# Moving transposes one slot, splitting the first feed-forward pair and reordering one block in an mLSTM and Fourier-mixing kernel

## The chip, the core and the metric

The kernel runs on one core of a Trainium2 chip. The metric is the device time of that core in microseconds, from one launch to its end. The engines are named as the profile names them: PE is TensorE's matrix multiply and PEld its weight load, DVE is VectorE, ACT is ScalarE, POOL is GpSimd, and SP issues the transfers (all of them here).

## The reference

All tensors are float32, with 4 batches, 8 heads, 768 tokens and a head width of 40. The first half is an mLSTM cell, a recurrence over the tokens whose output for each token and head is a gated read of a decaying 40 x 40 state:

```python
C = f_stab * C + i_stab * outer(v_t, k_t);  n = f_stab * n + i_stab * k_t
y[t] = sigmoid(o_t) * (C @ q_t) / max(|n . q_t|, 1)
```

The second half takes the 320 features of each token (8 heads of 40):

```python
u  = x + real(fft(fft(x, axis=seq), axis=feature))
un = (u - mean(u)) / sqrt(var(u) + 1e-6)
out = u + relu(un @ w_ch1) @ w_ch2          # 320 -> 1280 -> 320
```

## The kernel before

The tokens of a batch are cut into six chunks of 128. The mLSTM is computed chunk by chunk, as decayed attention inside a chunk and a state carried between chunks. `mlstm_scores` multiplies the keys and queries of a chunk into two PSUM banks (pool `ps_s`), `mlstm_exp` makes decay weights on ACT, POOL masks them, and `mlstm_weigh` multiplies the two on DVE. I call the PE work of one later chunk (read of the state, scores of the next, product with the values, new state) a chunk block.

The Fourier transform is done with matrices of cosines and sines. `mix_feat` leaves the transform of two chunks in a bank `pu`. Then for each chunk, in the order 0, 5, 1, 4, 2, 3:

- `mix_add` (DVE) adds the transform to x, giving u, and takes mean and variance. Chunks 2 and 3 read the same `pu`, as do 0 and 5, and 1 and 4.
- `mix_center` (ACT) writes u minus its mean into one of two buffers `uc`.
- `mix_turn` (PE, "a turn") transposes it in three 128 x 128 pieces into a bank `put`.
- `mix_turn_out` (ACT) copies that to `uT`, which the feed-forward product reads.

For batches 2 and 3 the banks are fixed by a table: the turns go to banks 3, 3, 3, 3, 2, 3 and the three `pu` sit in banks 3, 2, 2. So the fifth turn (chunk 2) takes the bank from which the adds of chunks 2 and 3 read.

The feed-forward of batch 0 is written plainly. `mlp_in` makes a pair of hidden blocks of 128 for three chunks at once: for each of the two blocks, two products with the 128-row parts of the weight and one with its 64-row tail, each 384 columns wide. For the later batches the feed-forward is done with seven block products in place of eight. `mlp_block` makes a hidden pair for all six chunks in four steps, and its hidden blocks get their relu in place on ACT (`mlp_relu_in_place`). `mlp_sums` and `hidden_sums` (DVE) prepare sums of operands. `mlp_out_pair` makes the output of one pair of chunks in four steps of two groups of five products, into the banks x and y, and after each group `residual` (DVE) adds the bank to u. For three pairs that gives twelve slots. I name them S0 to S11. They belong to one batch's feed-forward, and the mix of the next batch is spread over the same slots. The mix of batch 2 lies beside the output of batch 1, at about 222 to 275 us. The mix of batch 3 lies beside the output of batch 2, at about 318 to 360 us. The turns of those two mixes stand after S5, S6, S7, S8, S9 and S10.

The order of the work is written by hand. `at(slot, phase, fn)` puts a function into a table that is sorted by slot and phase, and each engine receives its instructions in that order and runs them in order. The phases in a slot are EVAC 0, FILL 1, MAIN 2 and FILL_PE 3. PSUM banks 0 to 3 of the pool `ps_m` are given out by `bank`, from the string `turn` in the early part and by the tables later. A tile that takes a bank waits for the last reader of the tile before it.

Between the mix of batch 0 and its feed-forward, at about 52 to 71 us, PE waits between the turns. There the kernel issues three `idle_products`, products of zeros, one after each of the first three turns. In the same stretch the weights arrive as 64-bit numbers and are turned to float32 in pieces: a load (SP), `take` (DVE), `convert` (ACT) and `join` (DVE). All of these share the in-order queues with the mix.

Of the kernel before, what the change touches and what calls it, by code (L numbers as in the profile page):

```python
# [10 lines left out]
FP = mybir.dt.float32  # L11
# [8 lines left out]
L = 128  # L20
NT = S // L
NP = H // 2
# [6 lines left out]
TG = NT // 2  # L29
# [21 lines left out]
def kernel(  # L51
# [14 lines left out]
    nc = tc.nc  # L66
# [13 lines left out]
    ps_h = pool("ps_h", 2, space=PSUM)  # L80
    ps_m = pool("ps_m", 1, space=PSUM)

    turn = iter("3210321032120312031230123012012301023130201320132013201320123021320321")

    def bank(name, shape, n=None):

        return ps_m.tile(shape, FP, name=name, tag=f"pm{next(turn) if n is None else n}")
# [34 lines left out]
    def at(slot, phase, fn, *args):  # L122
        plan.setdefault((slot, phase), []).append((fn, args))
# [7 lines left out]
    EVAC, FILL, MAIN, FILL_PE = range(4)  # L131


    def idle_products(n, first=False):
        pw = bank("pi", [L, 2 * L]) if first else ps_s.tile([L, 2 * L], FP, name="pi", tag="ps")
        for i in range(n):
            nc.tensor.matmul(pw, rest[:, 0:L], rest, start=True, stop=True, skip_group_check=True)


    def gates(gp):  # L140
# [16 lines left out]
        nc.vector.memset(ebias, -896.0 * 2.0**23)  # L157
        nc.gpsimd.memset(qk_bufs[0][:, 0], 0.0)
        nc.scalar.activation(out=warm, in_=rest[:, 0:1], func=AF.Exp)
        idle_products(3, True)  # L160
        mlstm_load(0, 0)
        make_identity(nc, ident)
        nc.gpsimd.memset(later_b, 0.0)
# [291 lines left out]
                nc.gpsimd.tensor_tensor(out=k.Cd[r] if b == 0 else k.C_next[r, :, m], in0=k.C[r, :, m], in1=d,  # L455
                                        op=OP.mult)

    def mlstm_scores(b, c):

        k = chunks[b, c]  # L460
        k.ps = [ps_s.tile([L, NP, L], FP, name=f"ps{hip}", tag="ps") for hip in range(2)]
        for p in range(NP):
            for hip in range(2):
                r = slice(hip * 64, hip * 64 + D)
                nc.tensor.matmul(k.ps[hip][:, p, :], k.qk[r, 1, p, :], k.qk[r, 0, p, :], start=True, stop=True)  # L465
# [87 lines left out]
    def plan_mlstm(b, s0, stride=3):  # L553
        for c in range(NT):
            s = s0 + stride * c
            if b > 0:
                t = 22 + 2 * c if b == 1 and c < 3 else s - 5
                at(t, FILL, mlstm_load, b, c)
                at(t, FILL, mlstm_load_max, b, c)
                at(t, FILL, mlstm_load_decay, b, c)  # L560
                at(s, FILL, mlstm_load_o, b, c)
            if (b, c) > (0, 0):
                at(s, FILL, mlstm_exp, b, c, 0)
                at(s + 1, FILL - 0.5, mlstm_exp, b, c, NP)
                last = (b, c) == (0, NT - 1)
                at(s - 1 if last else s, FILL_PE + (2.05 if last else 2), mlstm_scores, b, c)
                if b > 0:
                    at(s + 1, FILL, mlstm_mask, b, c)
            at(s, FILL, mlstm_scale_v, b, c)
            at(s if (b, c) == (0, 2) else s + 1, FILL + 0.1, mlstm_scale_q, b, c)  # L570
            at(s + 2, FILL, mlstm_decay, b, c)
            end = (b, c) == (0, NT - 1)
            at(s + 1 if end else s + 2, FILL - 0.4 if end else FILL, mlstm_weigh, b, c)
            at(s + 2 if end else s + 3, FILL_PE, mlstm_from_state, b, c)
            at(s + 2 if end else s + 3, FILL_PE + (2 if end else 3), mlstm_from_chunk, b, c)
            at(s + 3, FILL_PE + 3, mlstm_to_state, b, c)
            at(s + 3 if end else s + 4, FILL, mlstm_gather, b, c)
            if b == 0:
                t, x = ((8, 11), (11, 14), (13, 14), (14, 15.5), (17, 18), (18, 21))[c]
            else:  # L580
                t = s + (8, 8, 7, 5, 5, 5)[c]
                x = t + 1
            at(t, FILL_PE + ((2.5 if c < 4 else 1) if b == 0 else 1), mlstm_turn, b, c, b == 0 and c < 4)
            at(x, FILL + 0.05, mlstm_finish, b, c)
# [240 lines left out]
                at(t + 1, EVAC, mix_turn_out, b, c)  # L825


    def mlp_in(b, gr, f):


        k = mixes[b]
        u = [uT_bufs[gr][:, ch].rearrange("p c t -> p (c t)") for ch in range(3)]
        if f % 2 == 0:
            k.pm = [bank("pm", [L, TG * L]) for _ in range(2)]
        for i, ch in ((1, 1),) if f % 2 else ((0, 0), (0, 1), (1, 0)):
            f0 = (f // 2 * 2 + i) * L
            nc.tensor.matmul(k.pm[i], w1_sb[:, ch, f0:f0 + L], u[2 * ch], start=(ch == 0), stop=False)  # L837
        if f % 2:
            for i in range(2):
                r = slice(i * TAIL, (i + 1) * TAIL)  # L840
                nc.tensor.matmul(k.pm[i], w1t_sb[r, f // 2 * L:(f // 2 + 1) * L], u[1][r], start=False, stop=True)


    hid = {}
# [142 lines left out]
    def mlp_out_pair(b, n, step):  # L987

        k = mixes[b]
        half, first, last = NFF // 2, slice(0, HALF_D), slice(HALF_D, DM)  # L990
        c1, c2 = ORDER[TG + MLP_PAIRS[n][1]], ORDER[MLP_PAIRS[n][0]]
        if step == 0:
            k.po = [bank("po", [L, HALF_D], (n + j) % 2) for j in range(2)]
        x, y = k.po
        w = {(r, side): w2_sb[:, 1 - r:NFF:2, side * HALF_D:(side + 1) * HALF_D] for r in range(2) for side in range(2)}

        def product(po, a, w, start=False):
            for f in range(half):
                nc.tensor.matmul(po, a[:, f], w[:, f], start=start and f == 0, stop=f == half - 1, skip_group_check=True)  # L999

        def s(j):
            return hsum[f"S{j}"].rearrange("p (f t) -> p f t", t=L)

        if step == 0:
            product(x, pair_block(n, 1, 1), w[0, 0], True)
            residual(b, c1, first, x)
            product(y, pair_block(n, 1, 0), w[1, 0], True)
            residual(b, c1, first, y)
        elif step == 1:
            product(x, s(2), w2x["T2"])  # L1010
            residual(b, c1, last, x)
            product(y, s(1), w[0, 1], True)
            residual(b, c2, last, y)
        elif step == 2:
            product(x, s(3), w2x["T3"])
            residual(b, c2, last, x)
            product(y, s(4), w[1, 1])
            residual(b, c1, last, y)
            store(b, c1)
        else:  # L1020
            product(x, pair_block(n, 0, 0), w2x["T4"])
            residual(b, c2, first, x)
            store(b, c2)
# [3 lines left out]
    def plan_mlp(b, s):  # L1027
        groups = range(NT // TG)
        for i in range(NFF // 2) if b > 0 else ():
            for step in range(4):  # L1030
                at(s, MAIN, mlp_block, b, i, step)
                s += 1
            end = i == NFF // 2 - 1
            for n, (gr, f) in enumerate(((1, 2 * i + 1), (1, 2 * i), (0, 2 * i))):
                at(*((s, EVAC) if end else (s + n, MAIN + 0.5)), mlp_relu_in_place, gr, f)
        for gr in groups if b == 0 else ():
            for f in range(NFF):
                at(s, MAIN, mlp_in, b, gr, f)
                s += 1
                if f % 2:  # L1040
                    at(s, EVAC, mlp_relu, b, gr, f - 1)
                    at(s, EVAC, mlp_relu, b, gr, f)
        if b > 0:
            for j in range(1, 5):
                at(s - 1, FILL + 0.3 if j < 3 else FILL_PE + 0.3, hidden_sums, 0, (j,), 0, NFF // 2 - 1)
            at(s, EVAC, hidden_sums, 0, (1, 2, 3, 4), NFF // 2 - 1, NFF // 2)
        for n in range(TG) if b > 0 else ():
            for step in range(4):
                at(s, MAIN, mlp_out_pair, b, n, step)
                if n < TG - 1 and step > 1:  # L1050
                    for j in (2 * step - 3, 2 * step - 2):
                        at(s, MAIN + 0.6, hidden_sums, n + 1, (j,))
                s += 1
        for gr in groups if b == 0 else ():
            for i in range(TG):
                for half in range(2):
                    at(s, MAIN, mlp_out, b, gr, i, half)
                    s += 1
                at(s, EVAC, mlp_store, b, gr, i)
# [6 lines left out]
    def plan_batch(b, s_mlstm, s_mix, s_mlp):  # L1066
# [9 lines left out]
        else:  # L1076
            feat = [s_mix + c for c in ((3, 4, 6) if b == 1 else (3, 4, 7))]
            add = [s_mix + c for c in ((4, 4, 5, 6, 7, 7) if b == 1 else (4, 4, 5, 6, 8, 9))]
            turn = [s_mix + c for c in ((5, 6, 6) if b == 1 else (5, 6, 7))]
            late = [s_mix + c for c in ((7, 8, 8) if b == 1 else (8, 9, 10))]  # L1080
            at(s_mlp, EVAC + 0.5, mlp_sums)
        plan_mix(b, s_mix, done, feat, add, turn + late)
        at(s_mlp + NFF, FILL + 0.6, mix_rstd, b)
# [26 lines left out]
             (14, mlstm_load_o, 5), (23, None, 4)]  # L1110
    for s, load, c in early:
        at(s, FILL + 0.8, *((pieces[c].load,) if load is None else (load,) if c is None else (load, 0, c)))

    for s, phase, n in ((24, 5.5, 1), (25, 5.5, 1), (26, 5.5, 1)):
        at(s, FILL_PE + phase, idle_products, n)
    run(15)
    gates_pool.close()

# [109 lines left out]
```

## Time and profile before

| what | value |
|---|---|
| median of 8 runs | 427.81 us (427.05 to 429.07) |
| the profiled execution's own time | 427.83 us |
| its span, first to last instruction | 426.1 us |
| PE busy | 409.1 us, 96% of the span |
| DVE, ACT, POOL busy | 288.8, 189.9, 114.2 us |
| chain that ended last | 77% on PE, 10% on DVE, 5% on transfers |
| mean granted TensorE clock | 0.999 |

The busy share of PE counts pipelined products with modelled ends, so it does not tell how much PE could still be relieved. What PE waits for, and where, is read from the waits and the timeline. The profiled execution lies 0.02 us from the median of the runs, so sums made on it can be compared with the median directly.

### The profile page before, as it was taken

How to read it: one execution, taken by the hardware profiler on the slowest of the kernel's cores; microseconds unless marked ns; L12 is line 12 of the kernel's file. 1: busy time of each engine (PE TensorE's matmuls, PEld its weight loads, DVE VectorE, ACT ScalarE, POOL GpSimd, SP SyncE). 2: the span in 40 equal slices, each digit the busy share in tenths (PEclk: the TensorE clock that was granted, in tenths of full speed). 3: DMA queues.
4: the chain of work that ended last, by engine and by line, in shares of the span. 5: the costliest groups of instructions: out<-in, count | busy, mean ns of one | idle time of the engine just before them, and what ended most of it. 6: DMA issues, size and time to landing. Idle time of an engine off the chain costs nothing.

```text
span 426.1 us, 7994 instructions
## 1 busy us (share of the span) xinstructions
PE 409.1 (96%) x2966; PEld 302.2 (71%) x2966; DVE 288.8 (68%) x682; ACT 189.9 (45%) x493; POOL 114.2 (27%) x194
## 2 busy tenths in 40 slices
PE   8999999999899999999999999899999997999997
PEld 6877555666567778776459998776459996555996
DVE  8798885768885547778655768778654785334552
ACT  6986375575561233654464343454450122354000
POOL 5564201467432421250311431450300000020000
PEclk9999999999999999999999999999999999999999
DMA  7889397667664254267000725200000000000010
GB/s 221 268 217 345 111 269 233 199 196 224 194 178 148 70 139 144 79 189 229 8 0 2 211 84 170 85 18 1 0 2 0 32 32 32 0 2 0 15 46 32
DMA packets 20549, 47.14 MB, mean 111 GB/s; under 512 B 2784, under 2 KB 9312, under 8 KB 20384
## 3 DMA queue, kind: packets, MB, share of 16 engines
q1 hardware_dynamic: 20512, 46.65, 36.0%
q8 instruction: 23, 0.38, 0.4%
q14 instruction: 14, 0.11, 0.1%
HBM read 42.52 MB, written 4.11 MB: 109 GB/s over the span
## 4 chain that ended last, share of the span: by engine, by line
PE 77%; DVE 10%; DMA 5%; issue 3%; ACT 2%; POOL 1%; SPq 0%; DVEq 0%; POOLq 0%; ACTq 0%
PE po L999 18%; PE pm L897 17%; PE po L943 8%; DMA raw<-in_w 5%; PE ph L486 5%; PE ps L465 5%; PE pm L902 5%; PE ph L479 4%; PE pu L729 3%; PE px L535 2%; PE put L772 2%; DVE S L985 2%; PE pz L698 2%; PE pz L686 1%; PE pc L496 1%
## 5 line engine op out<-in xcount | busy, mean ns | idle before, releaser
L949 DVE SCALAR_TENSOR_TENSOR x<-po,rstd,x 128x160 f32<-128x160 f32 (+1 forms) x69 | 27.1, 395 | 44.5 <-PE po L999 37.8
L906 DVE TENSOR_TENSOR h<-h,pm 128x384 f32<-128x384 f32 x60 | 30.5, 550 | 33.0 <-ACT h L919 24.7
L443 POOL TENSOR_SCALAR_AFFINE_SELECT W<-W 128x1024 f32<-128x1024 f32 x18 | 21.4, 1191 | 91.8 <-ACT W L421 71.5
L421 ACT ACTIVATE W<-W,colT 128x128 f32<-128x128 f32 x144 | 45.1, 394 | 0.0
L943 PE MATMUL po<-w_sb,h 128*128 128x320 f32 x120 | 34.4, 435 | 0.0
L897 PE MATMUL pm<-uT,w_sb 128*128 128x384 f32 x90 | 32.8, 492 | 0.2 <-DVE uT L885 0.2
L777 ACT COPY uT<-put 128x384 f32<-128x384 f32 x24 | 11.3, 478 | 48.5 <-PE put L772 48.5
L471 DVE TENSOR_TENSOR W<-ps,W 128x512 f32<-128x512 f32 x48 | 30.7, 680 | 2.9 <-POOL W L443 2.7
L837 PE MATMUL pm<-uT,w_sb 128*128 128x384 f32 x80 | 29.9, 500 | 0.7 <-DVE x L749 0.5
L943 PEld LDWEIGHTS po<-w_sb,h 128*128 128x128 f32 x120 | 22.2, 190 | 9.5 <-issue 0.8
L465 PE MATMUL ps<-qk 40*128 40x128 f32 x384 | 28.3, 284 | 0.1
L999 PE MATMUL po<-T,S 128*128 128x160 f32 x180 | 27.8, 301 | 0.5 <-DVE x L949 0.4
L792 POOL TENSOR_TENSOR t<-rstd 128x6 f32<-128x6 f32 x12 | 3.0, 246 | 92.0 <-DVE v L790 91.3
L999 PE MATMUL po<-w_sb,h 128*128 128x160 f32 x180 | 26.2, 301 | 1.2 <-DVE h L906 1.2
L999 PEld LDWEIGHTS po<-T,S 128*128 128x128 f32 x180 | 25.5, 190 | 2.2 <-DVE x L949 1.4
L999 PEld LDWEIGHTS po<-w_sb,h 128*128 128x128 f32 x180 | 24.9, 190 | 2.8 <-DVE h L906 2.4
L465 PEld LDWEIGHTS ps<-qk 40*128 40x128 f32 x384 | 23.7, 187 | 4.4 <-issue 0.7
L431 POOL TENSOR_TENSOR qg<-qk,Gb 128x512 f32<-128x512 f32 x18 | 26.2, 1455 | 0.9 <-DMA so<-in_o 0.8
L486 PE MATMUL ph<-W,kvt 128*41 128x128 f32 x384 | 25.8, 277 | 0.0
L479 PEld LDWEIGHTS ph<-qg,C 128*128 128x128 f32 x160 | 20.0, 191 | 6.7 <-issue 2.5
L897 PEld LDWEIGHTS pm<-uT,w_sb 128*128 128x128 f32 x90 | 16.2, 190 | 10.9 <-DVE h L906 1.5
L936 ACT ACTIVATE h<-h 128x384 f32<-128x384 f32 x45 | 23.0, 524 | 1.5 <-DVE h L906 1.5
(207 smaller groups left out, 851.1 us busy)
## 6 DMA issues: line engine op xcount, KB each, us to landing
W<-M_d SPq DMA_DIRECT2D x18, 512.0 KB
kvt<-in_kv SPq DMA_DIRECT2D x24, 324.0 KB
qk<-in_qkT SPq DMA_DIRECT2D x48, 160.0 KB
raw<-in_w SPq DMA_DIRECT2D x10, 640.0 KB
Gb<-G_d SPq DMA_DIRECT2D x36, 128.0 KB
so<-in_o SPq DMA_DIRECT2D x24, 160.0 KB
out<-x SPq DMA_DIRECT2D x24, 160.0 KB
ds_sb<-in_dft_s SPq DMA_DIRECT2D x1, 1155.0 KB
```

Source lines behind the costliest of these rows:

```text
L421: nc.scalar.activation(out=k.W[:, h, :], in_=M, func=AF.Exp, scale=-1.0, bias=colT[:, c, 0, b * H + h:b * H + h + 1])
L431: nc.gpsimd.tensor_tensor(out=k.qg, in0=k.qk[:, 0], in1=k.Gb, op=OP.mult)
L465: nc.tensor.matmul(k.ps[hip][:, p, :], k.qk[r, 1, p, :], k.qk[r, 0, p, :], start=True, stop=True)
L471: nc.vector.tensor_tensor(out=Wv, in0=k.ps[hip], in1=Wv, op=OP.mult)
L479: nc.tensor.matmul(k.ph[:, p, :], k.C[:, p, :], k.qg[:, p, :], start=(p == 0), stop=False, skip_group_check=True)
L486: nc.tensor.matmul(k.ph[hip * 64:hip * 64 + D1, p, :], k.v1[:, 2 * p + hip, :], k.W[:, 2 * p + hip, :], start=(c == 0 and p == 0), stop=Tr ...
L837: nc.tensor.matmul(k.pm[i], w1_sb[:, ch, f0:f0 + L], u[2 * ch], start=(ch == 0), stop=False)
L897: nc.tensor.matmul(bank, w, u, start=start, stop=True, skip_group_check=True)
L906: nc.vector.tensor_tensor(out=h, in0=h, in1=bank, op=OP.add)
L943: nc.tensor.matmul(k.po, hidden(gr, f)[:, i * L:(i + 1) * L], w2_sb[:, f, :], start=(f == 0), stop=(f == NFF - 1))
L949: nc.vector.scalar_tensor_tensor(out=u, in0=po, scalar=k.rstd[:, c:c + 1], in1=u, op0=OP.mult, op1=OP.add)
L999: nc.tensor.matmul(po, a[:, f], w[:, f], start=start and f == 0, stop=f == half - 1, skip_group_check=True)
```

## The change

The turns of the mixes of batches 2 and 3 stand one slot later, after S6, S7, S8, S9, S10 and S10. On ACT their centering and copies move with them. In the mix of batch 2 this also brings four `mlstm_exp` instructions ahead of the first centering, and in both mixes the last two centerings come before the last two copies.

In step 0 of `mlp_out_pair` the ten products are reordered. First come four of the five x products, then two of y, then the last x product and its residual, and then the other three of y. The number of products and their sizes are the same. This happens nine times, in batches 1 to 3.

In the mix of batch 0 the three `idle_products` are gone. In place of the first two stand the scores of chunk 0 of batch 1, half after each of the first two turns. These scores had stood after the first hidden pair. The first hidden pair is split by columns: the part of the first two chunks (256 columns) is issued around the third turn, one product ahead of it and the rest behind it, and the part of the third chunk (128 columns) follows. The string `turn` is changed so that every tile keeps the bank it had.

The order of instructions on DVE, POOL and SP is unchanged.

```diff
-    turn = iter("3210321032120312031230123012012301023130201320132013201320123021320321")
+    turn = iter("3210321032120312031230123010122301023130201320132013201320123021320321")
...
-    def mlstm_scores(b, c):
+    def mlstm_scores(b, c, pairs=(0, NP)):
         k = chunks[b, c]
-        k.ps = [ps_s.tile([L, NP, L], FP, name=f"ps{hip}", tag="ps") for hip in range(2)]
-        for p in range(NP):
+        if pairs[0] == 0:
+            k.ps = [ps_s.tile([L, NP, L], FP, name=f"ps{hip}", tag="ps") for hip in range(2)]
+        for p in range(*pairs):
...
-                at(s - 1 if last else s, FILL_PE + (2.05 if last else 2), mlstm_scores, b, c)
+                if (b, c) == (1, 0):
+                    at(24, FILL_PE + 5.5, mlstm_scores, b, c, (0, NP // 2))
+                    at(25, FILL_PE + 5.5, mlstm_scores, b, c, (NP // 2, NP))
+                else:
+                    at(s - 1 if last else s, FILL_PE + (2.05 if last else 2), mlstm_scores, b, c)
...
-    def mlp_in(b, gr, f):
+    def mlp_in(b, gr, f, t=(0, TG * L), which=(0, 3)):
         k = mixes[b]
-        u = [uT_bufs[gr][:, ch].rearrange("p c t -> p (c t)") for ch in range(3)]
-        if f % 2 == 0:
+        t = slice(*t)
+        u = [uT_bufs[gr][:, ch].rearrange("p c t -> p (c t)")[:, t] for ch in range(3)]
+        if f % 2 == 0 and t.start == which[0] == 0:
             k.pm = [bank("pm", [L, TG * L]) for _ in range(2)]
-        for i, ch in ((1, 1),) if f % 2 else ((0, 0), (0, 1), (1, 0)):
+        for i, ch in ((1, 1),) if f % 2 else ((0, 0), (0, 1), (1, 0))[slice(*which)]:
...
-        def product(po, a, w, start=False):
-            for f in range(half):
+        def product(po, a, w, start=False, f0=0, f1=half):
+            for f in range(f0, f1):
...
         if step == 0:
-            product(x, pair_block(n, 1, 1), w[0, 0], True)
+            product(x, pair_block(n, 1, 1), w[0, 0], True, 0, half - 1)
+            product(y, pair_block(n, 1, 0), w[1, 0], True, 0, 2)
+            product(x, pair_block(n, 1, 1), w[0, 0], False, half - 1, half)
             residual(b, c1, first, x)
-            product(y, pair_block(n, 1, 0), w[1, 0], True)
+            product(y, pair_block(n, 1, 0), w[1, 0], False, 2, half)
             residual(b, c1, first, y)
...
             for f in range(NFF):
-                at(s, MAIN, mlp_in, b, gr, f)
+                two = (0, 2 * L)
+                if gr == 0 and f == 0:
+                    at(26, FILL_PE + 4.5, mlp_in, b, gr, f, two, (0, 1))
+                    at(26, FILL_PE + 5.5, mlp_in, b, gr, f, two, (1, 3))
+                    at(26, FILL_PE + 5.5, mlp_in, b, gr, f + 1, two)
+                at(s, MAIN, mlp_in, b, gr, f, (2 * L, TG * L) if gr == 0 and f < 2 else (0, TG * L))
...
-            turn = [s_mix + c for c in ((5, 6, 6) if b == 1 else (5, 6, 7))]
-            late = [s_mix + c for c in ((7, 8, 8) if b == 1 else (8, 9, 10))]
+            turn = [s_mix + c for c in ((5, 6, 6) if b == 1 else (6, 7, 8))]
+            late = [s_mix + c for c in ((7, 8, 8) if b == 1 else (9, 10, 10))]
...
-    for s, phase, n in ((24, 5.5, 1), (25, 5.5, 1), (26, 5.5, 1)):
-        at(s, FILL_PE + phase, idle_products, n)
```

More of the change, by code (lines that the diff above doesn't have):

```diff
@@ L131, with idle_products @@
     EVAC, FILL, MAIN, FILL_PE = range(4)
-    def idle_products(n, first=False):
-        pw = bank("pi", [L, 2 * L]) if first else ps_s.tile([L, 2 * L], FP, name="pi", tag="ps")
+    def idle_products(n):
+        pw = bank("pi", [L, 2 * L])
         for i in range(n):
@@ L159, in gates @@
         nc.scalar.activation(out=warm, in_=rest[:, 0:1], func=AF.Exp)
-        idle_products(3, True)
+        idle_products(3)
         mlstm_load(0, 0)
@@ L825, in plan_mix @@
                 at(t + 1, EVAC, mix_turn_out, b, c)
-    def mlp_in(b, gr, f):
+    def mlp_in(b, gr, f, t=(0, TG * L), which=(0, 3)):
         k = mixes[b]
-        u = [uT_bufs[gr][:, ch].rearrange("p c t -> p (c t)") for ch in range(3)]
-        if f % 2 == 0:
+        t = slice(*t)
+        u = [uT_bufs[gr][:, ch].rearrange("p c t -> p (c t)")[:, t] for ch in range(3)]
+        if f % 2 == 0 and t.start == which[0] == 0:
             k.pm = [bank("pm", [L, TG * L]) for _ in range(2)]
-        for i, ch in ((1, 1),) if f % 2 else ((0, 0), (0, 1), (1, 0)):
+        for i, ch in ((1, 1),) if f % 2 else ((0, 0), (0, 1), (1, 0))[slice(*which)]:
             f0 = (f // 2 * 2 + i) * L
-            nc.tensor.matmul(k.pm[i], w1_sb[:, ch, f0:f0 + L], u[2 * ch], start=(ch == 0), stop=False)
+            nc.tensor.matmul(k.pm[i][:, t], w1_sb[:, ch, f0:f0 + L], u[2 * ch], start=(ch == t.start == 0), stop=False,
+                             skip_group_check=True)
         if f % 2:
@@ L840, in mlp_in @@
                 r = slice(i * TAIL, (i + 1) * TAIL)
-                nc.tensor.matmul(k.pm[i], w1t_sb[r, f // 2 * L:(f // 2 + 1) * L], u[1][r], start=False, stop=True)
+                nc.tensor.matmul(k.pm[i][:, t], w1t_sb[r, f // 2 * L:(f // 2 + 1) * L], u[1][r], start=False, stop=True,
+                                 skip_group_check=True)
     hid = {}
```

## The prediction

> **What bounds the kernel now.** I read the page first, then PE's waits, then the timeline at each place that the change touches.
>
> ```profile
> PE 409.1 (96%) x2966; PEld 302.2 (71%) x2966; DVE 288.8 (68%) x682; ACT 189.9 (45%) x493; POOL 114.2 (27%) x194
> PE 77%; DVE 10%; DMA 5%; issue 3%; ACT 2%; POOL 1%; SPq 0%; DVEq 0%; POOLq 0%; ACTq 0%
> ```
>
> The chain that ended last runs through PE. So time is won only where PE, held in the chain, waits for another engine. PE's own waits name the place:
>
> ```profile
> engine line waited for: us in total, times, longest us
> PE put L772 <- DVE x L754: 4.3, 2, 2.1
> PE put L772 <- ACT uc L765: 1.3, 4, 0.4
> PE po L999 <- DVE h L906: 1.2, 2, 0.6
> ```
>
> The largest are two waits of a turn for an add, one in each late mix. The one of batch 3, with three lines of the same mix:
>
> ```profile
> 340.20 1.62 PE L999 MATMUL po<-T,S 128*128 128x160 f32 x10
> ...
> 354.50 0.31 DVE L754 TENSOR_TENSOR x<-x,pu 128x159 f32<-128x159 f32 x1
> 354.93 0.31 PEld L772 LDWEIGHTS put<-ident,uc 128*128 128x128 f32 x3 [2.34 <-issue]
> 354.96 0.52 PE L772 MATMUL put<-ident,uc 128*128 128x128 f32 x3 [2.13 <-DVE x L754]
> 355.38 0.18 DVE L757 BATCH_NORM_AGGREGATE x<-stats 128x2 f32<-128x6 f32 x1
> ```
>
> The reader is to see that the turn starts right after the L754 of 354.50. That add belongs to chunk 3, while the turn is of chunk 2, whose uc was ready at 352.58. The turn wants bank 2, which the add of chunk 3 still reads. Behind the turn, in PE's queue, stand S10 and S11, which don't need it.
>
> **The late turns, batch 3.** PE's starts before: S9 349.95, its end 352.67 (two groups of 1.36), fifth turn 354.96, S10 355.32, sixth turn 358.04, S11 358.36, end of S11 359.72. A turn costs PE 0.33 (343.02 to 343.35). After, step by step:
> 1. The first turn leaves its place ahead of S6. It cost nothing there: S6 started at 340.20, when DVE's residual (339.79) had read its bank. S6 stays at 340.20, and the turn now costs 0.33 behind it, where the second stood. The second, third and fourth move up one place each, so S7 to S9 keep their times.
> 2. The fourth turn stands behind S9, at 352.67. S10 follows at 353.05 in place of 355.32: 2.27 earlier. Its banks were read by the residuals of 351.79 and 352.87.
> 3. S10 ends at 355.77. The fifth turn goes at once, since bank 2 is free from about 354.9. The sixth needs chunk 3's uc: L757 at 355.38, ACT about 0.28 later (351.69 to 351.97), and PE about 0.66 after ACT's start (253.00 to 253.66 in the other mix), so 356.32, a wait of 0.2.
> 4. S11 starts at 356.65 instead of 358.36: **1.7 us won**. The next stage follows at once. Its DVE sums stand behind S11's residual (359.93, now 358.2), later than the last copy to uT (about 357.4), so its wait for them stays at 0.25.
>
> **The late turns, batch 2.** Here chunk blocks of batch 3 stand between. The waits removed are the fifth turn's (267.25 to 269.55, 2.3) and the second's for ACT (253.07 to 253.66, 0.6):
>
> ```profile
> 267.18 0.61 ACT L765 ACTIVATE uc<-x 128x384 f32<-128x384 f32 x1
> 269.09 0.31 DVE L754 TENSOR_TENSOR x<-x,pu 128x159 f32<-128x159 f32 x1
> 269.55 0.52 PE L772 MATMUL put<-ident,uc 128*128 128x128 f32 x3 [2.13 <-DVE x L754]
> ```
>
> After: S6 at 250.02, the first turn 252.74, S7 253.15, the transform and second turn to 257.1, S8 257.1 (before 258.05). S8's y waits for the residual of S7 on DVE, which in my chain ends at 258.0 against a need at 258.2, so it just fits. Then the chunk block (3.38, as 260.77 to 264.15) and the third turn, and S9 at 263.6. The fourth turn now stands behind four exps, the gather copies and a tanh on ACT, 2.1 from the first exp to uc (265.11 to 267.18). That gives uc at 266.3 and the turn at 266.95, where PE is ready at 266.35: a **new wait of 0.6**. Behind it are queued S10, two turns and S11. S10 runs 267.3 to 270.05, the fifth turn follows, the sixth at 270.4 (its uc from 269.3), the chunk transpose, and S11 at 271.2 against 273.39: **2.2 us won**. I checked the DVE chain: it starts 0.33 earlier with S6's residual and gains about 0.6 in the two sums of 255.24 and 256.28, which took 1.01 and 1.24 with POOL active, against 0.81 to 0.82 in batch 3 without it. POOL's work moves ahead, because four exps no longer wait for the first turn's copy. If those sums don't get shorter, S8 waits 0.4, and the gain is 1.8. I take 2.2, since the nearest quiet rows are of the same instruction. SP's loads behind these steps only come earlier.
>
> **The stretch before the first hidden pair.** Work leaves PE's path. After the first turns, 8 score instructions (16 take 1.09) replace 2 filler instructions (0.6 with their end): no change, since the turns wait for uc anyway. The first pair starts at 57.33, after the second copy to uT (56.82, 0.46), instead of 58.08. It puts one product (2 x 0.213, two thirds of the 0.32 that a 384-wide instruction adds) ahead of the third turn, which slips by 0.8. The pair is done near 61.0, while before pair and scores took until 62.6: **PE is 1.6 ahead**. But the next things in PE's queue are not ready:
>
> ```profile
> 63.73 0.61 ACT L765 ACTIVATE uc<-x 128x384 f32<-128x384 f32 x1
> 68.23 0.49 DVE L344 TENSOR_SCALAR e<-raw 128x640 uint32<-128x640 uint32 x1 [5.35 <-DMA raw<-in_w]
> 69.50 0.72 ACT L352 ACTIVATE m<-m 128x640 f32<-128x640 uint32 x1
> 70.13 0.85 ACT L850 ACTIVATE h<-pm 128x384 f32<-128x384 f32 x2
> 70.64 0.30 PEld L837 LDWEIGHTS pm<-uT,w_sb 128*128 128x128 f32 x2 [0.69 <-ACT h L850]
> ```
>
> The fourth turn waits for the uc of 63.73, at the end of an ACT queue that is full from 59.07. It can come 0.2 earlier at most. Then PE needs a bank of the second pair, whose relu (70.13) stands on ACT behind the converting of a weight piece, for which DVE waited until its load landed at 68.2. That load was issued at 60.11 and depends on no PE step, and SP's order is the same. So PE's lead ends at 70.64 whatever it is. I cost this part at **0**. The cover is the load; if it weren't there, up to 1.6 would be won. A loss is bounded by the third turn's 0.8, and its copy (to 58.8) still ends ahead of ACT's next step, 59.07.
>
> [...] The rows: the two empty stretches of 2.2 us in the late mixes left the granted clock at 1.00.
>
> ```profile
> 267.30:269.50 2.20, 0.12 (x1) 0.00 (x0) 1.88 (x8) 0.49 (x1) 2.12 (x4) 1.00 0.00 0
> 352.70:354.90 2.20, 0.13 (x1) 0.00 (x0) 1.86 (x8) 0.00 (x0) 0.00 (x0) 1.00 0.00 0
> ```
>
> The columns are length, PE, PEld, DVE, ACT and POOL busy, granted clock, transfers. [...] My longest new gap is about 1.1 us (63.1 to 64.2), shorter than those of the rows, so the sum is 0 by the rows. [...]
>
> **Step 0 of the output.** The last relu has time already:
>
> ```profile
> 317.55 1.48 DVE L906 TENSOR_TENSOR h<-h,pm 128x384 f32<-128x384 f32 x3
> 318.15 2.98 PE L999 MATMUL po<-w_sb,h 128*128 128x160 f32 x20 [0.58 <-DVE h L906]
> 318.59 1.35 ACT L936 ACTIVATE h<-h 128x384 f32<-128x384 f32 x3 [0.49 <-DVE h L906]
> ```
>
> The wait is the first x product's, for the first of three DVE adds (to 318.06), which reads its bank; the reordering leaves it. The fifth x product comes 8 x 0.136 later, at 319.24, and its relu ends at 319.1. Moving it back saves at most the 0.1 by which this group is longer than the 2.88 of others. In return x's residual comes 0.54 later and y starts 0.27 earlier. In the last stage x's residual (405.71) already stands behind DVE sums, and PE resumes on it at 406.14; the x product is done by 405.3. y would wait 0.07, inside that slack. Sum over nine places: **0**, bounds 0.3 won and 0.5 lost.
>
> **Sum.** 1.7 + 2.2 + 0 + 0 = 3.9. The profiled execution took 427.83 (span 426.1, 1.7 around it), 0.02 from the median 427.81. 427.83 - 3.9 = **423.9 us**.
>
> **The rivals.**
> - The first stretch gains too: the load is not the gate after all, because a pair 1.6 earlier lets ACT run ahead. For: PE's lead is real. Against: 68.23 and 70.13 above. 3.9 + 1.3: 422.6.
> - DVE or ACT becomes the bound in the late mixes. For: in batch 2 DVE runs without a break from 253.3 to 264.4, and my S8 fits by 0.2. Then waits of 0.5 to 1 return at S8, at the fourth turn and at S11; half the gain is kept: about 425.8.
> [...]
> - The turns don't move what they seem to: the order of instructions shows that they do, so only waits could undo it; gain within 0.2%, 427.5.
>
> **How the numbers follow.** Main case 0.63, first stretch too 0.13, half the gain 0.14, nothing 0.04, clock 0.06. About 0.2% (0.9 us) is what a measurement of this kernel tells from no change. The first three are faster by more: 0.90; same 0.04; slower 0.06. The range goes from 422.5 (first stretch gains) to 425.8 (half): it leaves out the last two cases and the tails.
>
> **What would show it.** PE's waits should have no turn waiting for L754 near 2.1; two turns a mix wait for ACT by 0.2 to 0.6. The sixth turn and S11 follow the fifth closely. From S6 to S11's end batch 3 takes 17.8 instead of 19.5. DVE's L344 near 68.2 and PE's third product of the third pair at 70.6 stay. Wrong would be: 70.6 coming earlier, a clock below 1 at 57 to 71, S8 or S11 of batch 2 waiting for DVE by more than 0.5, or PE's output stage after 393 changing its length.

## The result and the profile after

The changed kernel takes 423.66 us (median of 11 runs, 422.32 to 424.71). The kernel before took 427.65 us in the same comparison (32 runs, 426.08 to 429.52). The ratio is 0.9901, with a 95% interval of 0.9885 to 0.9917. That is 4.0 us less, where 3.9 was predicted.

The profiled execution took 422.95 us with a span of 421.2. The page says:

```profile
PE 408.2 (97%) x2972; PEld 302.5 (72%) x2972; DVE 287.7 (68%) x682; ACT 189.8 (45%) x493; POOL 112.8 (27%) x194
PE 76%; DVE 9%; DMA 7%; issue 3%; ACT 3%; POOL 2%; SPq 0%; POOLq 0%; ACTq 0%; DVEq 0%
```

PE is busy nearly as long as before (408.2 us against 409.1), while the span is 4.9 us shorter. PE's waits in the changed kernel:

```profile
PE put L778 <- ACT uc L771: 1.5, 4, 0.5
PE po L1008 <- DVE h L915: 1.2, 2, 0.6
PE po L1008 <- DVE x L958: 0.6, 2, 0.4
```

The row of 4.3 us, turns that wait for the add of L754 (now L760), is gone. What a turn still waits for is ACT, by 0.5 at most in this list. The mix of batch 3 in PE's timeline:

```profile
336.93 1.62 PE L1008 MATMUL po<-T,S 128*128 128x160 f32 x10 [0.26 <-DVE x L958]
...
351.13 1.52 PE L1008 MATMUL po<-w_sb,s_last 128*128 128x160 f32 x10
352.49 1.16 PE L778 MATMUL put<-ident,uc 128*128 128x128 f32 x6
353.48 1.52 PE L1008 MATMUL po<-T,h 128*128 128x160 f32 x10
354.84 1.45 PE L906 MATMUL pm<-uT,w_sb 128*128 128x384 f32 x4
```

The row of 336.93 is S6, and the one of 353.48 is S11. The fifth and sixth turns are the six instructions of 352.49. They take 0.99 together, where two turns without a wait take 0.66 (269.03 to 269.69 in batch 2), so the sixth waits about 0.3. From S6 to the end of S11 it is 17.91 us (336.93 to 354.84), against 19.52 before.

The mix of batch 2, on PE:

```profile
262.62 1.52 PE L1008 MATMUL po<-T,S 128*128 128x160 f32 x10
263.99 1.52 PE L1008 MATMUL po<-w_sb,S 128*128 128x160 f32 x10
265.93 0.55 PE L778 MATMUL put<-ident,uc 128*128 128x128 f32 x3 [0.43 <-ACT uc L771]
266.31 1.52 PE L1008 MATMUL po<-T,S 128*128 128x160 f32 x10
267.68 1.52 PE L1008 MATMUL po<-w_sb,s_last 128*128 128x160 f32 x10
269.03 0.82 PE L778 MATMUL put<-ident,uc 128*128 128x128 f32 x6
```

Where 2.3 us were empty before, the fourth turn now waits for its uc, which ACT starts at 265.27. S9's second group leaves PE free at 265.35, so this costs 0.58. From the first chunk block's read of the state to the third's it is 25.94 us (245.55 to 271.49), against 28.17 before (246.58 to 274.75).

Laid beside each other by PE's starts, the changed execution is ahead by 0.20 us before the first stretch (54.47 against 54.67), by 0.12 after it, and by 1.03 from 112 us on. Between lies a stretch from 97 to 112 us in which no order changed and PE waits for DVE and POOL. It differs from run to run: from the tail products near 94.6 to a chunk's read of the state near 111 it takes 16.85 us before and 15.95 in the changed kernel, but also 15.98 in the run with step 0 alone and 16.83 in the run with the late turns alone, which both have the order of before there. So I count its 0.9 as scatter: the two profiled executions are 4.88 apart, the medians 4.0. The mix of batch 2 then adds 2.23, and the mix of batch 3 adds 1.61. After that nothing changes.

### The profile page after: what moved, and what is told of

It reads as the page before. It is cut to its first block, busy times and chain, and to the rows that moved or that the text cites. A ratio compares the mean times of both kernels' runs of the same rounds, so it can differ in the third digit from the quotient of the medians.

```text
span 421.2 us, 8005 instructions
## 1 busy us (share of the span) xinstructions
PE 408.2 (97%) x2972; PEld 302.5 (72%) x2972; DVE 287.7 (68%) x682; ACT 189.8 (45%) x493; POOL 112.8 (27%) x194
## 4 chain that ended last, share of the span: by engine, by line
PE 76%; DVE 9%; DMA 7%; issue 3%; ACT 3%; POOL 2%; SPq 0%; POOLq 0%; ACTq 0%; DVEq 0%
PE po L1008 19%; PE pm L906 17%; PE po L952 8%; PE ps L466 5%; PE pm L911 5%; PE ph L487 4%; DMA raw<-in_w 4%; PE ph L480 3%; PE pu L735 3%; PE px L536 2%; PE pz L704 2%; PE put L778 2%; DMA kvt<-in_kv 1%; PE pz L692 1%; DMA qk<-in_qkT 1%
## 5 line engine op out<-in xcount | busy, mean ns | idle before, releaser
L906 PE MATMUL pm<-uT,w_sb 128*128 128x384 f32 x90 | 32.8, 492 | 0.2 <-DVE uT L894 0.2
L844 PE MATMUL pm<-uT,w_sb 128*128 128x384 f32 (+2 forms) x88 | 30.3, 471 | 1.2 <-DVE x L755 0.5
L525 ACT COPY h<-ph 41x512 f32<-41x512 f32 (+1 forms) x16 | 9.3, 583 | 35.7 <-PE ph L487 35.6
L431 POOL TENSOR_TENSOR qg<-qk,Gb 128x512 f32<-128x512 f32 x18 | 25.1, 1393 | 0.8 <-DMA Gb<-G_d 0.7
```

The source lines that it names most:

```text
L431: nc.gpsimd.tensor_tensor(out=k.qg, in0=k.qk[:, 0], in1=k.Gb, op=OP.mult)
L844: nc.tensor.matmul(k.pm[i][:, t], w1_sb[:, ch, f0:f0 + L], u[2 * ch], start=(ch == t.start == 0), stop=False, skip_group_check=True)
L906: nc.tensor.matmul(bank, w, u, start=start, stop=True, skip_group_check=True)
```

## The experiments

Each run is told with its own median. The medians of before beside them were 428.03 us (the first four below), 428.09 (the other bank, no products of zeros, and the two with the weight pieces later) and 427.83 (the two with waits filled, and the two with the centering earlier).

**The late turns alone.**

```diff
-            turn = [s_mix + c for c in ((5, 6, 6) if b == 1 else (5, 6, 7))]
-            late = [s_mix + c for c in ((7, 8, 8) if b == 1 else (8, 9, 10))]
+            turn = [s_mix + c for c in ((5, 6, 6) if b == 1 else (6, 7, 8))]
+            late = [s_mix + c for c in ((7, 8, 8) if b == 1 else (9, 10, 10))]
```

> The kernel before with the late turns alone, in the mixes of batches 2 and 3. Theory (the whole gain is the turns'): 3.9 us less than before, about 423.9, as for the full change; S6 to the end of S11 of batch 3 falls from 19.5 to 17.9 us, and the mix of batch 2 gives about 2.2 more. Rival (the first stretch or step 0 carries a part of the gain): less than 3.5 is won here, and the full change stays below it by the rest.

Measured: 423.95 us, ratio 0.9915 (0.9894 to 0.9937). The mix of batch 3 takes 17.91 us, and that of batch 2 25.88. By the medians that is 4.1 us, so the whole gain is that of the turns.

**The late turns in batch 3 alone.** Batch 2 keeps slots 5, 6, 7 and 8, 9, 10.

> The kernel before with the late turns in the mix of batch 3 alone. Theory: 1.6 to 1.7 us less than before, about 426.1; the mix of batch 2 keeps its turn that waits 2.1 for an add. Rival (the two mixes aren't additive, for instance because the earlier end of one is given back at a load): the sum of this and of batch 2's part differs from the run with both by more than 0.5.

Measured: 426.79 us, ratio 0.9967 (0.9952 to 0.9983), so 1.2 us by the medians and 1.4 by the ratio. Batch 3's mix takes 17.91 us again, so the trace gives 1.61. Batch 2's turn still waits 2.13. Nothing is given back, and the two mixes add up in the trace; the late turns of batch 2 alone were not run.

**The first stretch alone.** The scores stand where zeros were multiplied, the first pair is split, and the rest is as before.

> The kernel before with the first stretch's part alone (scores in place of the products of zeros, first pair split by columns). Theory: PE runs ahead by more than 1 us near 61 and has lost it at the third product of the third pair, which stays at 70.5 to 70.7; time the same, within 0.3 us. Rival A (the lead is kept): 1.3 us less, and that product near 69.3. Rival B (the clock falls with the filler gone): granted clock below 1 between 57 and 71 us, and the time longer.

Measured: 427.66 us, ratio 1.0007 (0.9986 to 1.0028). The second pair starts at 61.73 against 62.60 before, so PE's lead is 0.87 us, somewhat less than the 1 expected. The third product of the third pair starts at 70.77. No gain. The profile has no drop of the clock. 3 of the 14 executions have a mean clock of 0.995 or 0.996; where it dropped in them no trace shows, but before shows such clocks at least as often (below).

**Step 0 alone.**

> The kernel before with the reordered step 0 alone, at nine places. Theory: the wait there is of the first x product for the first of the three adds, which the reordering leaves; time the same, within 0.3 us, and every group of step 0 at most 0.1 shorter. Rival: y's three products now wait for nothing and the last relu was late, so nine times 0.1 or more is won, 0.9 us or more.

Measured: 427.84 us, ratio 1.0000 (0.9982 to 1.0018). The groups that wait for the first add take 2.98, as before. Two groups of the last stage take 3.06 and 3.07 in place of 2.88, as y now waits for a bank there (by 0.18, where the prediction had 0.07), yet from the first group of that stage to the end it is 33.12 us against 33.14. The slack that the prediction named covers it.

**Only another bank.** The turns are unmoved.

```diff
-    MIX = {"z": (2, 3), "zt": 2, "u": (3, 2, 2), "ut": (3, 3, 3, 3, 2, 3)}
+    MIX = {"z": (2, 3), "zt": 2, "u": (3, 2, 2), "ut": (3, 3, 3, 3, 3, 3)}
```

> The kernel before with its turns unmoved; one number of the table of banks is changed, so that the fifth turn of the mixes of batches 2 and 3 takes bank 3 in place of bank 2, from which the add of chunk 3 reads. Theory (the wait of 2.1 us is for the bank alone, and moving the turn a slot later only steps around it): the wait is gone here too, 1.7 us won in each of the two mixes, about 424.4; the second turn's wait for ACT in batch 2 stays, so this falls 0.5 short of the late turns. Rival (the fifth turn was bound by its own uc or by ACT as well, so that it had to move): a turn still waits 1 us or more, and less than 2 is won in all.

Measured: 424.04 us, ratio 0.9907 (0.9876 to 0.9938). The timeline of PE where 2.3 us were empty:

```profile
265.40 1.52 PE L999 MATMUL po<-w_sb,S 128*128 128x160 f32 x10
267.35 0.55 PE L772 MATMUL put<-ident,uc 128*128 128x128 f32 x3 [0.42 <-ACT uc L765]
267.73 1.52 PE L999 MATMUL po<-T,S 128*128 128x160 f32 x10
```

The fifth turn stands where it stood and no longer waits for the add. Batch 2's mix takes 26.55 us (1.62 won), and batch 3's takes 17.87 (1.65 won). This settles the cause. The wait was for the bank that the adds of chunks 2 and 3 read, and one digit removes it. The rival fell.

**No products of zeros, and nothing in their place.**

```diff
-    for s, phase, n in ((24, 5.5, 1), (25, 5.5, 1), (26, 5.5, 1)):
-        at(s, FILL_PE + phase, idle_products, n)
```

> The kernel before without the three products of zeros, and nothing in their place; the output is not touched by them. Theory (the clock does not need them): granted clock 1.00 at 52 to 72 us, the turns wait for uc as long as the fillers took, time the same within 0.3 us. [...]

Measured: 427.83 us, ratio 1.0021 (0.9996 to 1.0046). The median hides three groups: 13 of the 22 executions have a mean clock of 0.999 or 1.0 and a median of 426.94, 2 have 0.996 (428.54 and 431.19), and 7 have 0.987 or 0.988 and lie between 431.28 and 432.46. The profile caught one of the seven, with two drops of the clock. Its windows, the later drop first (columns as in the prediction):

```profile
269.35:272.75 3.40, 1.27 (x11) 1.13 (x10) 3.00 (x11) 1.08 (x4) 3.15 (x5) 1.00 0.09 32
54.30:57.70 3.40, 1.85 (x11) 0.93 (x9) 3.26 (x9) 2.58 (x5) 0.00 (x0) 1.00 1.03 273
57.70:61.10 3.40, 2.83 (x6) 1.50 (x5) 3.26 (x8) 2.18 (x5) 0.00 (x0) 0.50 1.06 252
61.10:64.50 3.40, 3.40 (x7) 1.50 (x7) 2.08 (x3) 0.92 (x4) 0.00 (x0) 0.50 1.02 251
```

An interval of 3.4 us in which PE was busy 1.85 us was followed by half clock. The next, at half clock, had 2.83 busy and was followed by half clock too, and the one after it, fully busy (3.40), was the last. The longest single gap ahead of the drop was 0.6 us (0.63, before the turn of 57.30). The price is read in its timeline:

```profile
58.43 5.49 PE L837 MATMUL pm<-uT,w_sb 128*128 128x384 f32 x8 [0.57 <-ACT uT L777]
...
271.65 0.52 PE L772 MATMUL put<-ident,uc 128*128 128x128 f32 x3 [2.13 <-DVE x L754]
272.01 2.16 PE L999 MATMUL po<-T,S 128*128 128x160 f32 x10
273.96 2.61 PE L999 MATMUL po<-w_sb,s_last 128*128 128x160 f32 x10
276.40 0.49 PE L772 MATMUL put<-ident,uc 128*128 128x128 f32 x3
```

The eight products of the first pair took 5.49 where they take 2.85. The second drop lies right behind the late mix's wait: S10 took 4.39 us (272.01 to 276.40), against 2.72 in the profile before. So this wait cost 1.7 us more than its empty time. My theory, that the clock does not need the zeros, fell for a third of the executions (7 of 22). The 13 without a drop lie 0.7 below those of before beside them (427.61), outside the expected 0.3; no run shows why.

**The wait of batch 2 filled.** There are 112 recorded executions of before beside these experiments. Of these, 78 have a mean clock of 0.999 or 1.0 and a median of 427.58 us. The other 34 have 0.995 or 0.996 and a median of 429.35. By my estimate 3.4 us at half clock, the length of the later drop above, take 0.004 off the mean of a span of 426 us, so these hold one drop each. The one profile of before has none.

```diff
+    at(92, FILL_PE - 0.15, idle_products, 4, True, 3)
```

The last number is the bank that the products write.

> The kernel before with four products of zeros (some 1.7 us) in PE's queue ahead of the fifth turn of batch 2, so that PE is busy in most of the wait of 2.1 to 2.3 us; the output is not touched by them, and the turn starts when it did. Theory (this wait costs twice: the empty time, in every execution, and now and then a stretch at half clock behind it): the usual executions stay at the time of before, 427.4 to 427.9; the executions with a mean clock of 0.995 or 0.996, a third of those of before, are gone, and the median falls by 0.3 to 0.6. Rival (the clock drops come from the wait of batch 3 or from elsewhere): their share stays a third.

Measured: 428.43 us, ratio 1.0010 (0.9994 to 1.0026). The timeline of PE shows the wait filled:

```profile
266.92 1.89 PE L137 MATMUL pi<-rest 128*128 128x256 f32 x8
269.21 0.52 PE L772 MATMUL put<-ident,uc 128*128 128x128 f32 x3 [0.41 <-DVE x L754]
```

The 13 executions without a drop have a median of 427.47, as have those of before beside them, so the zeros cost nothing. Still 9 of 22 have 0.995 or 0.996, and the median did not fall. My theory fell, and the rival held: another wait drops the clock as well.

**Both waits filled.**

```diff
+    at(92, FILL_PE - 0.15, idle_products, 4, True, 3)
+    at(124, FILL_PE - 0.15, idle_products, 4, True, 3)
```

> The kernel before with four products of zeros ahead of the fifth turn in both late mixes; the output is not touched by them. Theory (only the wait of batch 2 lets the clock drop): as with batch 2's alone. Rival (batch 3's does it as well): executions at 0.996 are left in the run with batch 2's alone, and gone here.

Measured: 427.35 us, ratio 0.9990 (0.9974 to 1.0006). None of 14 executions has a clock below 0.999, where three in ten would give four. So the drops of the kernel before come from these two waits. With batch 3's removed (the second experiment) 8 of 22 executions dropped, with batch 2's filled 9 of 22, and with both still there 34 of 112. Filling them wins back the drops but not the empty time, and the median stays at that of the undisturbed executions of before (427.47 beside this run). So my theory fell here too, and the rival held.

**The weight pieces later.** This and the next run try to keep the lead that the first stretch wins.

```diff
-    when += [((s, 0.7), (s + 1, 0.7), (s + 2, 0.6)) for s in (33, 36, 39, 42, 45)]
+    when += [((s, 0.7), (s + 1, 0.7), (s + 2, 0.6)) for s in (35, 38, 41, 44, 47)]
```

> The changed kernel with the conversion of the later weight pieces (take, convert, join) two slots later in each engine's order. Theory (what takes PE's lead away at 70.5 is the relu queued on ACT behind a piece whose load lands at 68.2): that wait is gone, and PE keeps the lead of 0.4 that it still has at the fourth turn, 0.3 more than the changed kernel, unless a later product meets its weights unready; about 423.4. Rival (the lead is lost to the mix's own chain, not to the load): the third product of the third pair still waits for a relu at 70.5.

Measured: 424.59 us, ratio 0.9929 (0.9902 to 0.9955). The wait at the third product is gone. The scores behind the pair start at 70.50 instead of 71.37, and PE's lead over the changed kernel grows to 1.56 at 75 us (0.28 of it from before the pair). Then two new waits take it back:

```profile
PE pc L497 <- DVE x L551: 2.0, 1, 2.0
...
PE pc L497 <- DVE v L791: 1.0, 1, 1.0
```

In DVE's timeline the cause of the first is seen. The join of a piece, whose last instruction is this L364, now stands ahead of the chunk's output L551 and makes it late:

```profile
101.84 1.24 DVE L364 TENSOR_TENSOR w_sb<-m,e 128x640 f32<-128x640 f32 x1
...
104.41 0.49 DVE L551 TENSOR_TENSOR x<-px,so 128x320 f32<-128x320 f32 x1
```

The piece was the gate at 70.5, as the theory said, but the predicted gain of 0.3 turned into new waits, and the median lies 0.9 above the changed kernel's. In 3 of 10 executions the clock is 0.996 besides.

**And the second exps behind the fourth centering.**

```diff
-                at(s + 1, FILL - 0.5, mlstm_exp, b, c, NP)
+                at(s + 1, FILL + 0.15 if (b, c) == (1, 0) else FILL - 0.5, mlstm_exp, b, c, NP)
```

> The kernel of the run before, with the second half of the decay weights' exps of the first chunk of batch 1 behind the fourth centering on ACT, ahead of which they stood. Theory (the fourth turn waits 0.5 for its uc only because ACT's queue is full from 59): that wait falls by half or more, and PE's lead after it is 0.8 to 1.0, so the time is 0.5 lower again, about 422.9, if the mask on POOL and the weighing on DVE that need these exps aren't late for the chunk. Rival (they are late): the chunk's product with the values waits for them by as much as was won, and the time is that of the run before.

Measured: 423.61 us, ratio 0.9915 (0.9886 to 0.9945). The fourth turn no longer waits (64.08). Among executions without a drop this is 1.1 below the run before (423.41 against 424.48), twice what was expected; the traces don't account for the rest. The new wait of 2.0 us near 103 stays, and in 4 of 9 executions the clock is 0.996. The profile is one of them: 105.46 to about 108.9 is at half clock, right behind that wait. Neither expectation named this.

**The centering earlier**, in the changed kernel, and then in the kernel before together with the other bank:

```diff
-            at(t, FILL + 0.1, mix_center, b, c)
+            at(t, FILL + 0.1 if b < 2 else FILL - 0.6, mix_center, b, c)
```

> The changed kernel with the centering of batches 2 and 3 ahead of the exps and copies of its slot on ACT. Theory: the fourth turn's wait of 0.4 in batch 2 goes, about 423.3. Rival (the exps that now come later are what a mask or a product waits for): the time stays at 423.7.

Measured: 422.92 us (5 runs, 422.17 to 423.28), ratio 0.9888 (0.9869 to 0.9906). The fourth turn no longer waits (265.64, right behind S9), but now the sixth waits some 0.3 for its uc: the fifth and sixth take 0.99 together (268.69 to 269.68), as in batch 3. So the mix takes 25.67 us, 0.27 less than in the changed kernel. It is the lowest median of all, but the intervals overlap, so the times alone don't show that it beats the changed kernel.

> The kernel before with the one number of the table of banks changed (fifth turn in bank 3), its turns unmoved, and the centering of batches 2 and 3 ahead of the exps and copies of its slot on ACT. Theory: the two waits of 0.4 for uc that are left in batch 2 go as well, 0.8 less than with the bank alone, about 423.2. Rival (the exps and copies that now come later are what a product or a mask waits for): the time stays at 424.0, with a new wait in the chunk blocks.

Measured: 424.19 us, ratio 0.9913 (0.9894 to 0.9932). Batch 2's mix takes 26.01 us, 0.54 less than with the bank alone. The two waits are gone, but the sixth turn now comes before its uc, for which ACT waits on DVE's statistics (L757):

```profile
270.91 0.55 PE L772 MATMUL put<-ident,uc 128*128 128x128 f32 x3 [0.45 <-ACT uc L765]
```

The time doesn't show the 0.5. What was expected did not come in full.

## Why the prediction was right

**Late turns, batch 3: 1.7 predicted, 1.61 measured** (17.8 predicted from S6 to the end of S11, 17.91 measured). The fifth turn follows S10 at once. The sixth waits for uc by about 0.3 instead of 0.2, which is the difference. In batch 2 only the fourth turn waits for ACT, so it is one such turn in each mix, where the prediction's list of signs had two. The reading of the wait as one for the bank, not for uc, is shown by the run with the other bank.

**Late turns, batch 2: 2.2 predicted, 2.23 measured.** The new wait of the fourth turn was predicted at 0.6 and is 0.58. S8 was to fit by 0.2, and it nearly does: its first group starts at 256.08, right behind the turn of 255.70, and its twenty products take 2.93 instead of 2.88. The two sums that were to shorten did:

```profile
253.92 0.79 DVE L994 TENSOR_TENSOR S<-h,h 128x640 f32<-128x640 f32 x1
254.75 0.82 DVE L994 TENSOR_TENSOR S<-S,h 128x640 f32<-128x640 f32 x1
```

They are DVE's timeline of the changed kernel, and took 1.01 and 1.24 before.

**First stretch: 0 predicted, nothing measured.** The timeline of the changed kernel, with PE's rows and ACT's:

```profile
57.67 0.49 PE L778 MATMUL put<-ident,uc 128*128 128x128 f32 x3
...
61.53 2.20 PE L844 MATMUL pm<-uT,w_sb 128*128 128x384 f32 x6
...
64.22 0.55 PE L778 MATMUL put<-ident,uc 128*128 128x128 f32 x3 [0.49 <-ACT uc L771]
...
69.38 0.72 ACT L352 ACTIVATE m<-m 128x640 f32<-128x640 uint32 x1
70.01 0.85 ACT L859 ACTIVATE h<-pm 128x384 f32<-128x384 f32 x2
70.53 0.91 PE L844 MATMUL pm<-uT,w_sb 128*128 128x384 f32 x2 [0.32 <-ACT h L859]
```

The kernel before has its second pair at

```profile
62.60 2.20 PE L837 MATMUL pm<-uT,w_sb 128*128 128x384 f32 x6
```

The third turn slipped by 0.7 (0.8 predicted). Where the second pair starts, PE was 1.1 us ahead, was down to 0.4 at the fourth turn, and had 0.1 left at 70.53, where the relu stands behind the piece. The run with the pieces later shows that this gate was the piece's. As 0.2 of this lead was there before the stretch, the stretch itself won 0.9 (0.87 in the run of it alone), not the 1.6 predicted. The prediction counted the split pair as no longer than the whole one, but it takes PE 4.06 us (57.14 to 61.53, less 0.33 for the turn) against 3.53 (58.08 to 61.61). This error did no harm, since the gate takes any lead.

**Step 0: 0 predicted, 0 measured**, by the run of it alone.

**The clock: the right number by a wrong reading.** The prediction costed the clock at 0 by two rows of the profile before in which the granted clock is 1.00. But these rows cover the empty stretches of 2.2 us themselves, and in a profile with a drop it came behind such a stretch: in the run without zeros, too, the row of 269.35 has 1.00, and half clock follows at 272.75. And although that profile has no drop behind its waits either, it is one execution. In 34 of 112 executions the clock did drop behind these same waits, as the run with both filled shows. The error was to take a single profile as proof that a gap of 2.2 us is harmless, and to compare single gaps rather than the busy share of an interval: the first drop of the run without zeros came with no gap above 0.6. The drops spoke for the change. It removes both waits, and with them the drops: none in the 12 executions of the changed kernel, nor in those of the turns alone, the other bank, or the two runs with earlier centering (23 together). 34 of 112 times 1.8 us (429.35 against 427.58) is some 0.5 us in the mean of before, which the sum did not contain. Set against the undisturbed executions of before alone, the changed kernel is 427.58 - 423.66 = 3.9 us faster, which is what the sum said. The step that failed is thus the rows' reading. That the sum still came out is in part luck: it was made on a profile without a drop, and the drops raise the median of before by only 0.1 to 0.5 (427.65 to 428.09).

The case that the prediction's chances call clock (0.06) did not come: no execution of the changed kernel has a mean clock below 0.999. But it was nearer than I thought. These are the windows of the changed kernel and of the kernel before, in this order, at the place where the run without zeros had 1.85:

```profile
54.00:57.40 3.40, 2.70 (x24) 1.93 (x24) 3.26 (x8) 2.39 (x5) 0.00 (x0) 1.00 0.94 269
```

```profile
54.00:57.40 3.40, 2.71 (x16) 1.59 (x15) 3.26 (x8) 2.58 (x5) 0.00 (x0) 1.00 0.97 291
```

The scores keep PE as busy as the zeros did. Had the change only deleted the zeros, I estimate from the run without them that 7 of 22 executions would have lost some 2.9 us (431.6 - 426.9, less 1.8 for the second drop): the slower case of those chances, in a part of the executions. The other rivals fell: the first stretch gained nothing by itself, S8 takes only 0.05 longer, and S11 doesn't wait for DVE.

## What to carry to other kernels

When an in-order engine waits for something that its instruction doesn't use, look at the buffer that it writes: here a turn with its data ready waited 2.1 us for another chunk's add, and a different bank number did nearly as much as moving six turns (424.04 against 423.95 us). Before work is gathered ahead of a wait, find the next thing in the queue that isn't ready, or the lead is lost there (here 1.1 us at 61.53 had become 0.1 at 70.53). Judge the clock by PE's busy share and over many executions: here half clock came behind stretches of 3.4 us with PE busy 37 to 54%, and 34 of 112 executions of the kernel before have a mean clock of 0.995 or 0.996, so its one profile with the clock at 1.00 proved little.

## What the runs showed of the hardware

In the run without zeros, the granted clock dropped from 1.00 to 0.50 right after an interval of 3.4 us with PE busy 1.85 us (54.3 to 57.7), and again after one with 1.27 (269.35 to 272.75). In the profile with the pieces and exps later it was 1.36 (102.1 to 105.5). So PE was not idle ahead of the drops: it was busy for 37 to 54% of those intervals. One drop lasted 3.41 us (272.75 to 276.16) and one 6.83 (57.71 to 64.54). In the profile with the pieces and exps later it was 3.41 (105.46 to 108.87). The interval of 3.4 us is the length of the shorter drops. In the profile of the changed kernel the emptiest 3.4 us between 1 and 411 us, wherever the interval is laid, have 2.57 busy (39.4 to 42.8), and none of its 12 executions has a mean clock below 0.999. What lies between 1.85 and 2.57 is open.

A low busy share did not bring a drop every time. The profile before has 1.27 busy from 267.2 to 270.6 and again from 352.6 to 356.0, and the clock stayed at 1.00 (0.999 in the mean). The same program drops in some executions and not in others: 34 of 112 of the kernel before, and 9 of 22 without zeros. No run shows what decides this, nor why no execution of before has two drops (the lowest mean clock is 0.995, and two would give 0.992 by the estimate above), although it has two such waits.
